# A reordered prologue in a linear-attention plus MLP kernel: tile transposes by DMA, early weight transposes, small loads on ACT's queue

## The chip, the cores and the metric

The kernel runs on one core of one Trainium2 chip. The metric is the device time of one execution in microseconds (us). All matmul inputs are bf16. The engines are PE (TensorE; PEld is its weight load), DVE (VectorE), ACT (ScalarE), POOL (GpSimd) and SP (SyncE), which here only issues DMAs. "SPq" and "ACTq" in the profile are DMA issues in the instruction streams of SP and ACT. Executions of one kernel do not all agree here: the kernel before has runs at about 185.8, 187.5 and 189 us, so runs carry a state (slow when a run is over 1.5% above the fastest of the same kernel, else fast), and comparisons use fast runs.

## The reference, cut to what matters

S = 2048 rows, D = 448 columns, H = 16 heads of 28, F = 1792. Branch A is linear attention with a softmax feature map, branch B a gated mixer and an MLP. Both start from the layer norm of the same x.

```python
xn = _layernorm(x)
# A: q, k, v = xn @ wqkv; per head pq = q @ w_phi, pk = k @ w_phi; phi = [softmax(p), softmax(-p)]
#    kv = phi_k^T v;  o = (phi_q kv) / (phi_q z + 1e-6);  A = o @ wo
# B: h = gelu(layernorm(xn) @ w1); shift four column groups along S; x1 = xn + hs @ w2
#    B = x1 + gelu(layernorm(x1) @ w3) @ w4
return x + A + B
```

The kernel folds w_phi into the q and k parts of wqkv: wpk = wk @ blockdiag(w_phi), and wpq likewise. For that it needs the q and k weights transposed (by DMA transposes from DRAM) and w_phi as a block-diagonal tile `bd` in SBUF.

## The kernel before

Each engine plays its own operations in order.

The prologue before the first exponential works in 16 tiles of 128 rows. It loads, normalizes (statistics on DVE, the power on POOL), transposes each tile into `xnT`, and computes V, the first MLP matmul (w1, gelu) and the folds.

```python
        R.ew(pool, "memset", bd[:, :], 0.0)
        load_x(0, 1)
        load_x(1, 1, "ACT")
        ...
        load_lap(wv, A_wqkv[:, 896:1344], ("ACT", "SP"))
        load_x(4, 2)
        load_x(6, 2)
        load_x(8, 4)
        load_x(12, 4)
        for q in range(4):                       # four loads of 6.1 KB, all on SP
            R.dma(bd[DH * q:DH * q + DH, :].rearrange("e (c f) -> e c f", c=NC)[:, :, DH * q:DH * q + DH],
                  A_w_phi.rearrange("(c q) e f -> q e c f", q=4)[q])
        for t in (1, 0):                         # weight transposes
            for c in range(NC):
                e0 = t * D + CR * c
                R.dma_t(wT[:, t, c, 0:D], A_wqkv[:, e0:e0 + 128])
        ...
        load_lap(w1, B_w1, ("ACT", "ACT"))
        ...
        def xn_T(i, b):                          # PE transpose of a tile, evacuated by ACT
            ...
        def xn_Td(i):                            # DMA transpose of a tile, issued by SP
            R.dma_t(xnT[:, :, 128 * i:128 * i + 128], xn[:, i, :])
```

Tiles 0 to 11 go through `xn_T`, tiles 12 to 15 through `xn_Td`. A list `play([...])` sets the order on PE: `V` are V matmuls, `W` are w1 matmuls, `FO` are folds, `v_out` evacuates V, and `spin` are matmuls that only keep PE busy. Each `W` or `FO` first half fills PSUM banks, and the second half finishes them and is evacuated.

The softmax here doesn't subtract the row's maximum and nothing guards it: scores larger than these inputs give would overflow.

Of the kernel before, what the change touches and what calls it, by code (L numbers as in the profile page):

```python
# [5 lines left out]
ACT = mybir.ActivationFunctionType  # L6
# [217 lines left out]
def bass_parallel_sum__linear_kernel_hedgehog__mixer_s_mlp__prompt_kernel(  # L224
    nc, A_x, A_wqkv, A_w_phi, A_wo, B_x, B_w1, B_w2, B_w3, B_w4, out,
):
    _, S, D = A_x.shape
    H, DH = A_w_phi.shape[0], A_w_phi.shape[1]
    F = B_w3.shape[1]
    assert (S, D, H, DH, F) == (2048, 448, 16, 28, 1792)  # L230
    NT, NG, KC, NC, NM, FC, HP = 16, 4, 4, 4, 4, 14, 32
    CR = 112
# [5 lines left out]
    with es:  # L238
        R = Recorder(nc, es)
# [17 lines left out]
        for b in range(4):  # L257
            t = es.enter_context(nc.psum_tensor("bank%d%d" % (2 * b, 2 * b + 1), [128, 1024], F32))
            R.track(t, 4096, psum=True)
            pairs.append(t)  # L260
        banks = [pairs[b // 2][:, 512 * (b % 2):512 * (b % 2) + 512] for b in range(8)]
# [7 lines left out]
        hT = view(hT_r, NM * HW).rearrange("p (m s) -> p m s", m=NM)  # L269
# [11 lines left out]
        wpk = new("wpk", KC * D).rearrange("p (c d) -> p c d", c=KC)  # L281
# [8 lines left out]
        bd = view(g_r, D)  # L290
# [50 lines left out]
        def load_x(i, n, eng="SP"):  # L341
            R.dma(xtok[:, i:i + n, :], x2d[128 * i:128 * (i + n), :].rearrange("(j p) d -> p j d", p=128), eng)
# [5 lines left out]
        def load_lap(dst, src, engs=("SP", "SP")):  # L348
            for h in range(2):
                R.dma(dst[:, 2 * h:2 * h + 2, :], src[192 * h:192 * h + 256, :].rearrange("(c p) d -> p c d", p=128), engs[h])  # L350
# [6 lines left out]
        load_lap(wv, A_wqkv[:, 896:1344], ("ACT", "SP"))  # L357
        load_x(4, 2)
        load_x(6, 2)
        load_x(8, 4)  # L360
        load_x(12, 4)
        for q in range(4):
            R.dma(bd[DH * q:DH * q + DH, :].rearrange("e (c f) -> e c f", c=NC)[:, :, DH * q:DH * q + DH],
                  A_w_phi.rearrange("(c q) e f -> q e c f", q=4)[q])
        for t in (1, 0):
            for c in range(NC):
                e0 = t * D + CR * c
                R.dma_t(wT[:, t, c, 0:D], A_wqkv[:, e0:e0 + 128])

        def load_rest():  # L370
            R.dma(w2[0:CR, :, :], B_w2.rearrange("(m p) d -> p m d", p=CR))
            load_lap(w3, B_w3)
            load_lap(wo, A_wo)
            R.dma(w4[:, :, :], B_w4.rearrange("(c p) d -> p c d", p=128))
# [2 lines left out]

        R.op("ACT", lambda e: e.preload_act_table_set("gelu_apprx_tanh_and_others"), [], [])
        load_lap(w1, B_w1, ("ACT", "ACT"))
        R.ew(pool, "memset", ident[:, :], 0.0)  # L380
        R.op(pool, lambda e: e.affine_select(ident[:, :], ident[:, :], pattern=[[-1, 128]],
                                             compare_op=ALU.not_equal, fill=1.0, base=0, channel_multiplier=1),
# [8 lines left out]
        def late_3():  # L391
            R.ew(pool, "memset", kvq[:, :, :], 0.0)
            R.ew(pool, "memset", wpq.rearrange("p c (h e) -> p (c h) e", e=HP)[:, :, DH:HP], 0.0)
            R.ew(pool, "memset", phik.rearrange("p t g e -> p (t g) e")[:, :, DH:HP], 0.0)
# [31 lines left out]
        def ln1_stats(a, n, neg):  # L426
            for i in range(a, a + n):
                ln_stats(st, mv, xtok, i)
            ln_scale(mv, rs, a, n, neg)

        def ln1_apply(eng, i):
            ln_apply(eng, halves(xn[:, i, :]), lap(xtok[:, i, :]), mv, rs, i)
# [7 lines left out]
        def fold_pair(t, m, b):  # L440
            def side(k, hi):
                r, c0, c1 = (slice(64, CR), 2 * DH, CR) if hi else (slice(0, 64), 0, 3 * DH)
                return [(banks[2 * b + k][:, CR * c + c0:CR * c + c1],
                         wT[r, t, c, START[m + k]:START[m + k] + 128], bd[r, CR * c + c0:CR * c + c1])
                        for c in range(NC)]

            def late():
                row_pairs(side(1, 0), side(0, 1))
                for k in range(2):
                    a = banks[2 * b + k]  # L450
                    if t:
                        R.ew(dve, "tensor_copy", wpk[:, m + k, :], a[:, 0:D])
                        continue
                    for j in range(2):
                        R.ew(dve, "tensor_copy",
                             wpq[:, m + k, :].rearrange("p (c j h e) -> p c j h e", c=NC, j=2, h=2)[:, :, j, :, 0:DH],
                             a[:, 224 * j:224 * j + 224].rearrange("p (c h e) -> p c h e", c=NC, h=2))
            return lambda: row_pairs(side(0, 0), side(1, 1), True), late
# [9 lines left out]
        def xn_Td(i):  # L468
            R.dma_t(xnT[:, :, 128 * i:128 * i + 128], xn[:, i, :])

        def two(b):
            return pairs[b // 2].rearrange("p (b e) -> p b e", b=2)
# [3 lines left out]
        def row_pairs(first, second, start=False):  # L476
            for s, (p, q) in enumerate(zip(first, second)):
                for out, lhs, rhs in (p, q):
                    R.mm(out, lhs, rhs, start and s == 0, False)

        def lap_pair(outs, lhs, rhs):
            def side(k, rows, kcs):
                return [(outs[k], lhs(k, kc, *rows), rhs(k, kc, *rows)) for kc in kcs]
            return (lambda: row_pairs(side(0, LO, (0, 1, 2, 3)), side(1, HI, (0, 1, 2, 3)), True),
                    lambda: row_pairs(side(1, LO, (0, 1, 3)), side(0, HI, (0, 2, 3))))
# [11 lines left out]
        def v_pair(i, b):  # L497
            return lap_pair([banks[2 * b + k][:, 0:D] for k in range(2)],
                            lambda k, kc, lo, hi: xnT[lo:hi, kc, 128 * (i + k):128 * (i + k) + 128],
                            lambda k, kc, lo, hi: wv[lo:hi, kc, :])  # L500
# [7 lines left out]
                R.ew(dve, "tensor_copy", vd, vs)  # L508

        def w1_pair(g, m, b):  # L510
            p = lap_pair([banks[2 * b + k][0:CR, :] for k in range(2)],
                         lambda k, kc, lo, hi: w1[lo:hi, kc, CR * (m + k):CR * (m + k) + CR],
                         lambda k, kc, lo, hi: xnT[lo:hi, kc, 512 * g:512 * g + 512])

            def late():
                p[1]()
                R.act(hT[0:CR, m:m + 2, 2 + 512 * g:2 + 512 * g + 512], two(2 * b)[0:CR, :, :], ACT.Gelu_apprx_tanh)
            return p[0], late

        def w2_pair(i, b):  # L520
            def side(k, lo, hi):
# [178 lines left out]
        def play(fs):  # L700
            for f in fs:
                f[0](*f[1:])

        for i in range(8):
            ln1_stats(i, 1, 0)
            if i not in (0, 4):
                ln1_apply(dve, i - 1)
            if i == 3:
                ln1_apply(dve, 3)

        def ln1_two(i):
            ln1_stats(i, 2, 1)
            ln1_apply(pool, i)
            ln1_apply(dve, i - 1)

        ln1_two(8)
        ln1_two(10)

        def ln1_rest():
            ln1_two(12)  # L720
            ln1_two(14)
            ln1_apply(dve, NT - 1)
            for i in range(12, 16):
                xn_Td(i)
            load_rest()
            late_3()

        vps = {i: v_pair(i, b) for i, b in ((0, 2), (2, 3), (4, 3), (6, 2), (8, 3), (10, 2))}
        wps = {(g, m): w1_pair(g, m, b) for g, m, b in ((0, 0, 0), (0, 2, 1), (1, 0, 0), (1, 2, 1), (2, 0, 0),
                                                        (2, 2, 1), (3, 0, 0), (3, 2, 3))}  # L730
        fps = {(t, m): fold_pair(t, m, b) for t, m, b in ((1, 0, 2), (1, 2, 3), (0, 0, 2), (0, 2, 1))}

        def V(i, k):
            return (vps[i][k],)

        def W(g, m, k):
            return (wps[g, m][k],)

        def FO(t, m, k):
            return (fps[t, m][k],)  # L740

        spin(19, 256)
        play([(xn_T, 0, 0), (spin, 4, 128), (xn_T, 1, 1), V(0, 0), (xn_T, 2, 0), V(0, 1), (v_out, 0, 2), (xn_T, 3, 1),
              V(2, 0), W(0, 0, 0), V(2, 1), (v_out, 2, 3), (xn_T, 4, 2), W(0, 2, 0), (xn_T, 5, 3), W(0, 0, 1),
              (xn_T, 6, 2), W(0, 2, 1), (xn_T, 7, 3),
              V(4, 0), V(6, 0), V(4, 1), (v_out, 4, 3), V(6, 1), (v_out, 6, 2, "DVE"), (ln1_rest,),
              W(1, 0, 0), (xn_T, 8, 3), W(1, 2, 0), (xn_T, 9, 2), W(1, 0, 1), (xn_T, 10, 3), W(1, 2, 1), (xn_T, 11, 2),
              V(8, 0), V(10, 0), V(8, 1), (v_out, 8, 3), V(10, 1), (v_out, 10, 2, "DVE"),
              W(2, 0, 0), W(2, 2, 0), W(2, 0, 1), FO(1, 0, 0), W(2, 2, 1), FO(1, 2, 0), FO(1, 0, 1), FO(0, 2, 0),
              FO(1, 2, 1), FO(0, 0, 0), FO(0, 2, 1), W(3, 0, 0), FO(0, 0, 1), W(3, 2, 0), W(3, 0, 1), W(3, 2, 1)])  # L750

        def w2_norm(i):
            for j in (i, i + 1):
# [7 lines left out]
        for ps in range(8):  # L761
            k, q = k_pair(2 * ps, 1), q_pair(ps // 2, 2 * (ps % 2), 0)
            kind, i = side[ps]
# [115 lines left out]
```

## Time and profile before

| | kernel before |
|---|---|
| time, median of 3 runs before the prediction | 187.62 us (187.59 to 189.05) |
| span of the profiled run | 184.9 us |
| PE busy | 173.3 us, 94% |
| ACT's first activation (timeline) | 5.84 us |
| first exponential (timeline) | 41.06 us |

These are lines of the profile's page of the kernel before: the span, busy time by engine, and the busy tenths of PE and the granted PE clock in tenths of full speed, in 40 slices of 4.6 us.

```profile
span 184.9 us, 5069 instructions
PE 173.3 (94%) x2193; PEld 101.1 (55%) x2193; DVE 112.6 (61%) x282; ACT 81.7 (44%) x91; POOL 96.5 (52%) x140
PE   7787879899999999999999999999999999999993
PEclk9879999999999999999999999999999999999999
```

Apart from the last slice, every slice in which PE is busy for less than 90% is among the first eight, the prologue. Behind it PE is nearly full, so what the prologue loses or wins moves the end of the kernel.

The windows view of the kernel before gives, for PE in each stretch (us): length, busy time and instructions, granted clock, DMA share and GB/s.

```profile
6.00:9.00 3.00, 2.22 (x25) 0.79 1.07 370
9.00:12.00 3.00, 2.08 (x22) 0.65 0.58 192
```

The clock is halved for one stretch of 3.4 us, from 7.96 to 11.37 us in the trace's clock records.

The timeline of the kernel before shows start, length, engine, line, operation, output <- input; in brackets the idle time before and what ended it.

```profile
2.18 1.00 ACTq L221 DMA_DIRECT2D w<-in_B_w_dram  x2
4.87 10.26 SPq L221 DMA_DIRECT2D g_tok<-in_A_w_phi_dram  x4
5.84 0.60 ACT L211 ACTIVATE xnT<-bank 128x512 bf16<-128x512 bf16 x1 [2.40 <-PE bank L207]
15.17 11.16 SPq L218 DMA_TRANSPOSE hi<-in_A_wqkv_dram  x8
41.06 1.73 ACT L211 ACTIVATE phik<-bank 128x896 bf16<-128x896 f32 x2
```

And this is a line of the waits of SP's DMA queue: who waited for what, us in total, times, longest.

```profile
SPq L221 <- DMA g_tok<-in_A_w_phi_dram: 8.7, 3, 6.3
```

The tile `bd` lives in the buffer `g_tok`. The four small w_phi loads occupy SP's stream for 10.26 us, though one issue takes only about 0.32 us: 8.7 us of it are waits of each load for the one before. The loads write disjoint partitions (0-27, 28-55, 56-83, 84-111), but neighbours share a 32-byte grain and a 64-partition block, so the tracker orders them.

### The profile page before, as it was taken

To read this page: it belongs to the slowest core of one execution; us is meant where nothing else is said; L and a number is where in the kernel's file an instruction comes from. 1 tells how busy PE (TensorE), PEld (TensorE's weight loads), DVE (VectorE), ACT (ScalarE), POOL (GpSimd) and SP (SyncE) were. 2 spreads that over 40 slices of the span, in tenths; PEclk is the share of its full clock that TensorE was granted. 3 is DMA by queue.
4 is the path that set the end of the run, shared out by engine and by line. 5 is a ranking of instruction groups with operands and counts; after the bars stand their busy time and mean duration, and the time that the engine had idled before them with its cause. 6 is when DMAs were issued, how large, how long until landed. Compare 5 with 4: busy or idle time off the path is not lost.

```text
span 184.9 us, 5069 instructions
## 1 busy us (share of the span) xinstructions
PE 173.3 (94%) x2193; PEld 101.1 (55%) x2193; DVE 112.6 (61%) x282; ACT 81.7 (44%) x91; POOL 96.5 (52%) x140
## 2 busy tenths in 40 slices
PE   7787879899999999999999999999999999999993
PEld 5344445695566977666544555455554545545451
DVE  5796183758889969762477695452744527464521
ACT  2248382489976977683524332221322214224000
POOL 3667158002869989993054938762170621722740
PEclk9879999999999999999999999999999999999999
DMA  5931444898000111113001346212622120211321
GB/s 130 362 107 31 96 80 91 270 386 302 8 5 0 32 28 32 28 32 85 0 4 32 59 88 57 78 32 78 88 58 80 30 78 4 82 28 28 82 82 48
DMA packets 33022, 14.88 MB, mean 80 GB/s; under 512 B 24744, under 2 KB 32488, under 8 KB 33000
## 3 DMA queue, kind: packets, MB, share of 16 engines
q1 hardware_dynamic: 31752, 13.58, 29.4%
q10 hardware_dynamic: 1248, 0.98, 1.6%
q8 instruction: 17, 0.28, 0.6%
q14 instruction: 5, 0.04, 0.1%
HBM read 7.08 MB, written 1.84 MB: 48 GB/s over the span
## 4 chain that ended last, share of the span: by engine, by line
PE 75%; DVE 13%; ACT 7%; issue 2%; POOL 1%; DVEq 0%
PE bank L203 75%; ACT hT L211 4%; DVE xn L215 4%; DVE st L215 4%; DVE ksum L215 2%; ACT phik L211 1%; DVE mv L215 1%; ACT xnT L211 1%; POOL rs L215 1%; DVE rks L215 1%; DVE vaug L215 1%; ACT L211 1%; POOL mv L215 0%; PE bank L207 0%; DVEq L176 0%
## 5 line engine op out<-in xcount | busy, mean ns | idle before, releaser
L211 ACT ACTIVATE phik<-bank 128x1024 bf16<-128x1024 f32 (+1 forms) x44 | 42.4, 986 | 61.6 <-PE bank L203 61.6
L203 PE MATMUL bank<-gT,w 64*128 64x512 bf16 x392 | 50.5, 377 | 0.5 <-ACT phik L211 0.2
L215 DVE TENSOR_TENSOR vaug<-bank,vaug 128x464 f32<-128x464 f32 (+3 forms) x65 | 32.6, 512 | 24.0 <-PE bank L203 22.3
L203 PE MATMUL bank<-w,phik 64*128 64x448 bf16 (+1 forms) x420 | 45.0, 349 | 0.1
L215 POOL TENSOR_TENSOR xnT<-vaug 128x196 bf16<-128x196 f32 (+1 forms) x32 | 18.1, 585 | 47.6 <-DVE vaug L215 47.6
L203 PEld LDWEIGHTS bank<-w,phik 64*128 64x128 bf16 (+1 forms) x420 | 21.7, 94 | 21.7 <-PE bank L203 0.5
L215 POOL TENSOR_TENSOR phik<-phik,rks 128x896 bf16<-128x896 bf16 x16 | 26.8, 1699 | 9.9 <-DVE rks L215 9.9
L203 PEld LDWEIGHTS bank<-gT,w 64*128 64x128 bf16 x392 | 18.4, 94 | 18.3 <-ACT phik L211 1.6
L203 PE MATMUL bank<-wv,xnT 64*128 64x448 bf16 x112 | 15.2, 375 | 4.8 <-ACT xnT L211 4.4
L215 DVE TENSOR_REDUCE ksum<-phik 128x32 f32<-128x896 bf16 x16 | 16.8, 1049 | 0.0
L215 POOL TENSOR_TENSOR vaug<-xn,xtok 128x448 f32<-128x448 bf16 x16 | 16.2, 1030 | 1.2 <-DVE vaug L215 1.2
L215 DVE TENSOR_TENSOR xn<-bank,xn 128x256 bf16<-128x256 f32 (+1 forms) x32 | 10.2, 382 | 10.7 <-PE bank L203 10.7
L203 PE MATMUL bank<-w,hT 64*128 64x448 bf16 (+1 forms) x128 | 16.3, 349 | 0.2 <-DVE xn L215 0.2
L203 PE MATMUL bank<-xnT,wpq 64*128 64x512 bf16 x112 | 15.9, 376 | 0.0
L215 DVE RECIPROCAL vaug<-bank 128x16 f32<-128x16 f32 x16 | 4.1, 257 | 17.9 <-PE bank L203 17.9
L203 PE MATMUL bank<-wpk,xnT 64*128 64x448 bf16 x112 | 14.6, 349 | 0.1
L203 PE MATMUL bank<-xnT,w 64*112 64x512 bf16 x112 | 14.4, 380 | 0.0
L203 PE MATMUL bank<-wo,xnT 64*128 64x448 bf16 (+1 forms) x106 | 13.4, 349 | 0.0
L215 POOL TENSOR_SCALAR g_tok<-xn,rs 128x512 bf16<-128x512 bf16 x16 | 12.1, 768 | 0.2
L215 POOL TENSOR_TENSOR rs<-mv,mhalf 128x1 f32<-128x1 f32 (+2 forms) x16 | 11.3, 705 | 1.3
L203 PEld LDWEIGHTS bank<-wv,xnT 64*128 64x128 bf16 x112 | 5.8, 97 | 10.6 <-ACT xnT L211 5.8
L203 PEld LDWEIGHTS bank<-w,hT 64*128 64x128 bf16 (+1 forms) x128 | 9.1, 94 | 4.4 <-DVE xn L215 1.2
(60 smaller groups left out, 181.1 us busy)
## 6 DMA issues: line engine op xcount, KB each, us to landing
w<-in_B_w_dram SPq DMA_DIRECT2D x2, 896.0 KB, 7.3
out_dram<-vaug SPq DMA_DIRECT2D x15, 112.0 KB, 1.9
w<-in_B_w_dram SPq DMA_DIRECT2D x1, 1568.0 KB, 11.2
xtok<-in_A_x_dram SPq DMA_DIRECT2D x2, 448.0 KB, 7.6
xtok<-in_A_x_dram SPq DMA_DIRECT2D x2, 224.0 KB, 6.1
w<-in_B_w_dram ACTq DMA_DIRECT2D x2, 224.0 KB, 6.3
wo<-in_A_wo_dram SPq DMA_DIRECT2D x2, 224.0 KB, 8.4
w<-in_B_w_dram SPq DMA_DIRECT2D x1, 392.0 KB, 3.8
```

Of the source, the lines that this page charges most:

```text
L203: self.op("PE", lambda e: e.matmul(out, lhsT, rhs, start=start, stop=stop, skip_group_check=True), [out], [lhsT, rhs], tile=self._tile(lhsT))
L211: self.op("ACT", lambda e: e.activation(out, in_, func, **kw), [out], [in_] + aps)
L215: self.op(eng, lambda e: getattr(e, name)(out, *args, **kw), [out], aps)
```

## The change

The intent: all of tiles 8 to 15 are transposed by DMA, which takes four transposes and four evacuations from PE and ACT; the weight transposes start early, so the folds can move forward; ACT's evacuations come in the order in which they are needed; and spins fill the first gaps. To free SP for the early transposes, the w_phi loads and x 8-11 move to ACT's queue. This is the core of the diff (bank numbers and the long play list are cut):

```diff
         load_x(6, 2)
-        load_x(8, 4)
-        load_x(12, 4)
-        for q in range(4):
-            R.dma(bd[DH * q:DH * q + DH, :]. ... ,
-                  A_w_phi.rearrange("(c q) e f -> q e c f", q=4)[q])
-        for t in (1, 0):
+        def load_wT(t):
             for c in range(NC):
                 ...
+        load_wT(1)
+        load_x(12, 4)
+        load_wT(0)
 ...
         load_lap(w1, B_w1, ("ACT", "ACT"))
+        for q in range(4):
+            R.dma(bd[DH * q:DH * q + DH, :]. ... ,
+                  A_w_phi.rearrange("(c q) e f -> q e c f", q=4)[q], "ACT")
+        load_x(8, 4, "ACT")
 ...
-                    if t:
-                        R.ew(dve, "tensor_copy", wpk[:, m + k, :], a[:, 0:D])
+                if t:
+                    R.act(wpk[:, m:m + 2, :], two(2 * b)[:, :, 0:D], ACT.Copy)
 ...
-        for i in range(8): ...        # layer norms 8-15 two tiles at a time (ln1_two)
-        def ln1_two(i):
-            ln1_stats(i, 2, 1); ln1_apply(pool, i); ln1_apply(dve, i - 1)
+        for i in range(NT):           # one tile at a time
+            by_pool = i >= 8 and i % 2 == 0
+            ln1_stats(i, 1, int(by_pool))
+            if by_pool:
+                ln1_apply(pool, i)
+            if i and not (i > 8 and i % 2):
+                ln1_apply(dve, i - 1)
+        ln1_apply(dve, NT - 1)
+        for i in range(8, NT):
+            xn_Td(i)
 ...
         spin(19, 256)
-        play([(xn_T, 0, 0), (spin, 4, 128), (xn_T, 1, 1), V(0, 0), ...
+        play([(xn_T, 0, 0), (spin, 3, 256), (xn_T, 1, 1), (spin, 2, 256), V(0, 0), ...
```

The order of ACT's instructions in the changed kernel, as built (not a profile), shows the w_phi loads and their waits ahead of the first evacuation. D19 to D21 are the completions of the first three:

```
5 L221 DMACopy g_tok<-in_A_w_phi_dram 28x4x28 [waits s_POOL]
6 L221 DMACopy g_tok<-in_A_w_phi_dram 28x4x28 [waits s_D19]
7 L221 DMACopy g_tok<-in_A_w_phi_dram 28x4x28 [waits s_D20]
8 L221 DMACopy g_tok<-in_A_w_phi_dram 28x4x28 [waits s_D21]
9 L221 DMACopy xtok<-in_A_x_dram 128x4x448
10 L211 Activation xnT<-bank01 128x4x128 [waits s_PE]
```

More of the change, by code (lines that the diff above doesn't have):

```diff
@@ L359, in bass_parallel_sum__linear_kernel_hedgehog__mixer_s_mlp__prompt_kernel @@
         load_x(6, 2)
-        load_x(8, 4)
-        load_x(12, 4)
-        for q in range(4):
-            R.dma(bd[DH * q:DH * q + DH, :].rearrange("e (c f) -> e c f", c=NC)[:, :, DH * q:DH * q + DH],
-                  A_w_phi.rearrange("(c q) e f -> q e c f", q=4)[q])
-        for t in (1, 0):
+        def load_wT(t):
             for c in range(NC):
@@ L379, in bass_parallel_sum__linear_kernel_hedgehog__mixer_s_mlp__prompt_kernel @@
         load_lap(w1, B_w1, ("ACT", "ACT"))
+        for q in range(4):
+            R.dma(bd[DH * q:DH * q + DH, :].rearrange("e (c f) -> e c f", c=NC)[:, :, DH * q:DH * q + DH],
+                  A_w_phi.rearrange("(c q) e f -> q e c f", q=4)[q], "ACT")
+        load_x(8, 4, "ACT")
         R.ew(pool, "memset", ident[:, :], 0.0)
@@ L448, in late @@
                 row_pairs(side(1, 0), side(0, 1))
+                if t:
+                    R.act(wpk[:, m:m + 2, :], two(2 * b)[:, :, 0:D], ACT.Copy)
+                    return
                 for k in range(2):
                     a = banks[2 * b + k]
-                    if t:
-                        R.ew(dve, "tensor_copy", wpk[:, m + k, :], a[:, 0:D])
-                        continue
                     for j in range(2):
@@ L510, in w1_pair, with w1_out @@
         def w1_pair(g, m, b):
-            p = lap_pair([banks[2 * b + k][0:CR, :] for k in range(2)],
+            return lap_pair([banks[2 * b + k][0:CR, :] for k in range(2)],
                          lambda k, kc, lo, hi: w1[lo:hi, kc, CR * (m + k):CR * (m + k) + CR],
                          lambda k, kc, lo, hi: xnT[lo:hi, kc, 512 * g:512 * g + 512])
-            def late():
-                p[1]()
-                R.act(hT[0:CR, m:m + 2, 2 + 512 * g:2 + 512 * g + 512], two(2 * b)[0:CR, :, :], ACT.Gelu_apprx_tanh)
-            return p[0], late
+        def w1_out(g, m, b):
+            R.act(hT[0:CR, m:m + 2, 2 + 512 * g:2 + 512 * g + 512], two(2 * b)[0:CR, :, :], ACT.Gelu_apprx_tanh)
         def w2_pair(i, b):
@@ L702, in play @@
                 f[0](*f[1:])
-        for i in range(8):
-            ln1_stats(i, 1, 0)
-            if i not in (0, 4):
-                ln1_apply(dve, i - 1)
-            if i == 3:
-                ln1_apply(dve, 3)
-        def ln1_two(i):
-            ln1_stats(i, 2, 1)
-            ln1_apply(pool, i)
-            ln1_apply(dve, i - 1)
-        ln1_two(8)
-        ln1_two(10)
-        def ln1_rest():
-            ln1_two(12)
-            ln1_two(14)
-            ln1_apply(dve, NT - 1)
-            for i in range(12, 16):
-                xn_Td(i)
-            load_rest()
-            late_3()
-        vps = {i: v_pair(i, b) for i, b in ((0, 2), (2, 3), (4, 3), (6, 2), (8, 3), (10, 2))}
-        wps = {(g, m): w1_pair(g, m, b) for g, m, b in ((0, 0, 0), (0, 2, 1), (1, 0, 0), (1, 2, 1), (2, 0, 0),
-                                                        (2, 2, 1), (3, 0, 0), (3, 2, 3))}
-        fps = {(t, m): fold_pair(t, m, b) for t, m, b in ((1, 0, 2), (1, 2, 3), (0, 0, 2), (0, 2, 1))}
+        for i in range(NT):
[4 more added lines that the diff above has]
+            if i and not (i > 8 and i % 2):
+                ln1_apply(dve, i - 1)
+        ln1_apply(dve, NT - 1)
+        for i in range(8, NT):
+            xn_Td(i)
+        load_rest()
+        late_3()
+        vps = {i: v_pair(i, b) for i, b in ((0, 2), (2, 3), (4, 3), (6, 2), (8, 2), (10, 3))}
+        wps = {(g, m): w1_pair(g, m, b) for g, m, b in ((0, 0, 0), (0, 2, 1), (1, 0, 0), (1, 2, 1), (2, 0, 2),
+                                                        (2, 2, 0), (3, 0, 2), (3, 2, 3))}
+        fps = {(t, m): fold_pair(t, m, b) for t, m, b in ((1, 0, 0), (1, 2, 1), (0, 0, 3), (0, 2, 1))}
         def V(i, k):
@@ L742, in bass_parallel_sum__linear_kernel_hedgehog__mixer_s_mlp__prompt_kernel @@
         spin(19, 256)
-        play([(xn_T, 0, 0), (spin, 4, 128), (xn_T, 1, 1), V(0, 0), (xn_T, 2, 0), V(0, 1), (v_out, 0, 2), (xn_T, 3, 1),
-              V(2, 0), W(0, 0, 0), V(2, 1), (v_out, 2, 3), (xn_T, 4, 2), W(0, 2, 0), (xn_T, 5, 3), W(0, 0, 1),
-              (xn_T, 6, 2), W(0, 2, 1), (xn_T, 7, 3),
-              V(4, 0), V(6, 0), V(4, 1), (v_out, 4, 3), V(6, 1), (v_out, 6, 2, "DVE"), (ln1_rest,),
-              W(1, 0, 0), (xn_T, 8, 3), W(1, 2, 0), (xn_T, 9, 2), W(1, 0, 1), (xn_T, 10, 3), W(1, 2, 1), (xn_T, 11, 2),
-              V(8, 0), V(10, 0), V(8, 1), (v_out, 8, 3), V(10, 1), (v_out, 10, 2, "DVE"),
-              W(2, 0, 0), W(2, 2, 0), W(2, 0, 1), FO(1, 0, 0), W(2, 2, 1), FO(1, 2, 0), FO(1, 0, 1), FO(0, 2, 0),
-              FO(1, 2, 1), FO(0, 0, 0), FO(0, 2, 1), W(3, 0, 0), FO(0, 0, 1), W(3, 2, 0), W(3, 0, 1), W(3, 2, 1)])
+        play([(xn_T, 0, 0), (spin, 3, 256), (xn_T, 1, 1), (spin, 2, 256), V(0, 0), (xn_T, 2, 0), V(0, 1), (xn_T, 3, 1),
+              (spin, 2, 256), V(2, 0), (v_out, 0, 2), W(0, 0, 0), V(2, 1), (v_out, 2, 3), W(0, 2, 0), (xn_T, 4, 2), W(0, 0, 1),
+              (xn_T, 5, 2), W(0, 2, 1), (xn_T, 6, 2), V(4, 0), (xn_T, 7, 2), V(4, 1), (w1_out, 0, 0, 0), V(6, 0), (w1_out, 0, 2, 1),
+              (v_out, 4, 3), W(1, 0, 0), V(6, 1), (v_out, 6, 2), W(1, 2, 0), W(1, 0, 1), (w1_out, 1, 0, 0), W(1, 2, 1),
+              (w1_out, 1, 2, 1), V(8, 0), FO(1, 0, 0), V(8, 1), (v_out, 8, 2), FO(1, 2, 0), FO(1, 0, 1), FO(1, 2, 1),
+              V(10, 0), W(2, 0, 0), V(10, 1), (v_out, 10, 3), W(2, 2, 0), FO(0, 2, 0), W(2, 0, 1), (w1_out, 2, 0, 2),
+              FO(0, 0, 0), W(2, 2, 1), (w1_out, 2, 2, 0), FO(0, 2, 1), W(3, 0, 0), FO(0, 0, 1), W(3, 2, 0),
+              W(3, 0, 1), (w1_out, 3, 0, 2), W(3, 2, 1), (w1_out, 3, 2, 3)])
         def w2_norm(i):
```

## The prediction

> **What bounds the kernel.** PE is busy 173.3 of 184.9 us (page, busy table). From 42.8 us on it has almost no gaps: 138.2 us busy of 142.2 (windows view). The change touches only the prologue up to the first exponentials at 41.06 us (timeline). From 5 to 42.8 us PE is busy 31.3 of 37.8 us, so at most 6.5 us of idling, plus about 1.7 us lost to the half clock (granted clock 0.79 and 0.65 between 6 and 12 us), can be won. The chain of waits runs over layer norms until 15.4 us, then over alternating ACT evacuations (0.60 us transposes, 1.02 us gelus) and PE.
>
> **What the change removes.** Four PE transposes of tiles (8 matmuls, 0.29 us each, 1.2 us of PE) with four ACT evacuations (0.60 us each, 2.4 us); two DVE casts of V (1.09 us) and four of wpk (0.58 us) move to ACT, as 2 x 0.92 us and about 2 x 0.95 us. Evacuations of tiles 4-7 no longer stand behind gelus, layer norms 12-15 no longer behind V casts; the SP queue issues the weight transposes (1.2-1.3 us each) from about 3.5 instead of 15.2 us. Alone this might win 3 us.
>
> **What it adds.** The four small w_phi loads move from the SP queue to ACT, ahead of ACT's first evacuation. Each waits for the landing of the one before: the instruction order shows the waits in ACT's stream. Before, these waits held SP 8.7 us (6.3 + 1.2 + 1.2; waits view of the DMA queue). The Trainium skill, "DMA: Bandwidth & Descriptors", Anatomy of one DMA, says that not DMA engines but the issuing sequencer waits on semaphores; the trace agrees, SP issued nothing meanwhile. Now ACT stands still. The first load lies behind w1 on ACT's queue, whose data end at 9.1 us (DMA records); the dependent loads then take about 1.5 us each. ACT issues the fourth near 12.3, then x 8-11, and makes its first evacuation near 13 us instead of 5.84. PE needs two evacuations for its first V matmul: about 14.3 instead of 7.0 us. After that idling the clock should be halved for 3 to 6 us (Trainium skill, "TensorE: Matmul & The Clock Gate", Part 1: an idle window of about 3.4 us throttles; this trace shows one).
>
> **Sum (estimates from trace durations).** PE work left at 14.3 us: 6 transposes 1.8, V 6 x 1.41, w1 8 x 1.63, folds 4 x 0.8 = 26.5 us; plus 2 us half clock, plus 1 us waits on ACT/DVE (wpq copies 0.31 us each before the last w1 pair): the last w1 matmul ends at 43.8 instead of 38.4 us. Behind it PE is the bound and the delay is kept. Predicted +5.3 us: 193 us, range 189.5 to 196. Chances: faster by over 2% 0.08, within 2% 0.20, slower by over 2% 0.72.
>
> **What would show it.** Right: ACT's first activation at 12-14.5 us, waits of ACT's queue on w_phi landings of 8-9 us, a PE gap of 5 us or more from about 7 us, clock 0.5 somewhere in 10-20 us, first exponential at 45-47.5 us, a rigid shift after. Transposes of tiles 8-15 land in time. Wrong: first activation before 8 us, PE dense from 7 us, first exponential before 39 us.
>
> **What would make it wrong.** Landings of w_phi faster than on SP; gaps in the new order smaller than I count; or tile transposes landing late, which would make it worse.

## More of the kernel before

A `Recorder` collects every operation in program order, with the bytes it reads and writes, and works out the semaphore waits.

The part that matters here is how the bytes are named: 32-byte grains in a row, but only two blocks of 64 partitions.

```python
GRAIN = 32
...
        p0 = (ap.offset * esz) // row_bytes
        p1 = p0 + dims[0][1]
        halves = [h for h in (0, 1) if p0 < 64 * h + 64 and p1 > 64 * h]
        keys = set()
        for s in starts:
            for b in range(s // GRAIN, (s + run - 1) // GRAIN + 1):
                for h in halves:
                    keys.add((name, b, h))
...
            for fn, todo, src, dma in self.stream[eng]:
                for f, i in todo:
                    e.wait_ge(get(f), 16 if f[0] == "D" and f[1:].isdigit() else self.marked[f][i])
                ins = fn(e)
```

## The result, and the profile after

The changed kernel takes 194.22 us (median of 4 runs, 194.14 to 195.13); the kernel before took 187.61 us in the same rounds (186.14 to 189.05). The ratio is 1.0391, 95% interval 1.0321 to 1.046. Here and below a ratio is the mean time of one kernel's fast runs over that of the other's fast runs of the same rounds, so not quite the ratio of the medians.

The page of the changed kernel, the same lines as before (slices are 4.8 us):

```profile
span 192.3 us, 5016 instructions
PE 175.4 (91%) x2164; PEld 101.4 (53%) x2164; DVE 110.1 (57%) x276; ACT 83.0 (43%) x91; POOL 99.1 (52%) x148
PE   7304999989999999999999999999999999999994
PEclk9855699999999999999999999999999999999999
```

PE is busy for 0.3, 0.0 and 0.4 of slices 2 to 4, and the clock is low from the third slice to the fifth. From there on the two kernels look alike. The windows of the changed kernel say the same in us:

```profile
6.00:9.00 3.00, 0.83 (x13) 0.94 1.45 260
9.00:12.00 3.00, 0.00 (x0) 0.50 1.06 201
12.00:15.00 3.00, 0.00 (x0) 0.50 0.82 198
15.00:19.00 4.00, 1.87 (x12) 0.50 0.58 142
19.00:23.00 4.00, 4.00 (x37) 0.59 0.03 8
```

The timeline of the changed kernel, with the lines that answer to those shown of before:

```profile
3.16 6.13 SPq L218 DMA_TRANSPOSE hi<-in_A_wqkv_dram  x4
3.24 12.76 ACTq L221 DMA_DIRECT2D g_tok<-in_A_w_phi_dram  x4
16.48 1.08 ACT L211 ACTIVATE xnT<-bank 128x512 bf16<-128x512 bf16 x2 [13.04 <-DMA g_tok<-in_A_w_phi_dram]
17.13 2.16 PE L203 MATMUL bank<-wv,xnT 64*128 64x448 bf16 x8 [9.97 <-ACT xnT L211]
48.53 1.73 ACT L211 ACTIVATE phik<-bank 128x896 bf16<-128x896 f32 x2
```

The four loads hold ACT from 3.24 to 16.0 us. ACT's first evacuation comes at 16.48 instead of 5.84 us, and PE, which has nothing to multiply before two tiles are evacuated, stands for 9.97 us. The first exponential is 7.47 us later than before (48.53 against 41.06), and so is the end: the spans differ by 7.4 us. (The medians differ by 6.6 us; the profiled run of the kernel before took 187.03 us, a little less than its median.)

The chain that ended last, in the changed kernel (start, length, what), follows exactly these landings:

```profile
3.24 7.43 DMA g_tok<-in_A_w_phi_dram
10.69 3.16 DMA g_tok<-in_A_w_phi_dram
13.87 1.78 DMA g_tok<-in_A_w_phi_dram
16.48 0.60 ACT xnT L211
```

### The profile page after: what moved, and what is told of

It is laid out like the page before. It is cut to its first block, busy times and chain, and to the rows that moved or that the text cites. A ratio compares the mean times of both kernels' runs of the same rounds, so it can differ in the third digit from the quotient of the medians.

```text
span 192.3 us, 5016 instructions
## 1 busy us (share of the span) xinstructions
PE 175.4 (91%) x2164; PEld 101.4 (53%) x2164; DVE 110.1 (57%) x276; ACT 83.0 (43%) x91; POOL 99.1 (52%) x148
## 3 DMA queue, kind: packets, MB, share of 16 engines
q1 hardware_dynamic: 32896, 13.62, 29.5%
## 4 chain that ended last, share of the span: by engine, by line
PE 78%; DVE 8%; DMA 6%; ACT 4%; ACTq 1%; issue 1%; DVEq 0%
PE bank L203 77%; DMA g_tok<-in_A_w_phi_dram 6%; DVE xn L215 3%; DVE ksum L215 2%; ACT phik L211 1%; ACT hT L211 1%; ACTq L221 1%; DVE st L215 1%; PE bank L207 1%; DVE rks L215 1%; DVE wpq L215 1%; ACT L211 1%; ACT xnT L211 1%; DVE mv L215 0%; ACT L378 0%
## 5 line engine op out<-in xcount | busy, mean ns | idle before, releaser
L203 PE MATMUL bank<-wv,xnT 64*128 64x448 bf16 x112 | 16.3, 385 | 10.3 <-ACT xnT L211 10.0
L203 PE MATMUL bank<-xnT,w 64*112 64x512 bf16 x112 | 14.9, 381 | 1.1 <-DVE wpq L215 1.0
L203 PEld LDWEIGHTS bank<-wv,xnT 64*128 64x128 bf16 x112 | 6.5, 99 | 15.7 <-ACT xnT L211 11.2
L215 DVE BATCH_NORM_STATS2 st<-xtok 128x6 f32<-128x448 bf16 x16 | 9.8, 615 | 7.5 <-DMA xtok<-in_A_x_dram 7.5
L215 POOL TENSOR_TENSOR rs<-mv,mhalf 128x1 f32<-128x1 f32 (+1 forms) x20 | 12.9, 644 | 1.7
```

What stands on the lines that cost most here:

```text
L203: self.op("PE", lambda e: e.matmul(out, lhsT, rhs, start=start, stop=stop, skip_group_check=True), [out], [lhsT, rhs], tile=self._tile(lhsT))
L215: self.op(eng, lambda e: getattr(e, name)(out, *args, **kw), [out], aps)
```

## The experiments

Theory A: the chained loads in ACT's instruction stream are the loss. Rival B: the new order itself (banks, evacuations moved to ACT, tile transposes by DMA) costs the time. Theory C came up on the way: a short PE wait costs more than its length, because the half clock follows it. Every run was numerically correct. Each kernel that was timed in rounds was compared with runs of the kernel before on the same chip; medians of those runs were 187.18, 187.55 and 187.52 us in the three sets.

### 1. The changed kernel without the chain (a_nochain)

The loads write disjoint partitions, so the tracker only has to see that. This takes no true dependence away; every other wait of the changed kernel stays, except that the folds now wait on all four loads.

```diff
-GRAIN = 32
+GRAIN = 32; CUTS = ((0, 28), (28, 56), (56, 64), (64, 84), (84, 128))
-        halves = [h for h in (0, 1) if p0 < 64 * h + 64 and p1 > 64 * h]
+        halves = [h for h, (a, b) in enumerate(CUTS) if p0 < b and p1 > a]
```

> The changed kernel, with the four w_phi loads on ACT's queue made independent of one another (they write disjoint partitions; only the dependence tracker's 64-row blocks chained them). Theory A (the chained loads hold ACT's instruction stream): ACT's first activation at 5.5 to 6.5 us instead of 16.5, first V matmul near 7 us, first exponential at 38 to 39.5 us instead of 48.5, time 184 to 186.5 us, so below the kernel before. Rival B (the new order itself, with its bank turns, its evacuations on ACT or its late tile transposes, costs the time and the stall is recovered): ACT starts early, but the time stays above 189 us, with the PE gaps moved to later waits.

Measured: 188.07 us (187.06 to 189.42), ratio to the kernel before 1.0075 (1.0004 to 1.0146). This is some 6 us below the changed kernel (two sets of rounds), but no win over the kernel before. Both theories were half right. The stall is gone, but the timeline shows a new wait later, and the windows show what follows it:

```profile
6.65 1.09 ACT L211 ACTIVATE xnT<-bank 128x512 bf16<-128x512 bf16 x2 [3.21 <-POOL mv L215]
17.26 13.20 SPq L218 DMA_TRANSPOSE xnT<-xn  x8
31.93 1.19 PE L203 MATMUL bank<-xnT,w 64*112 64x512 bf16 x8 [2.55 <-DMA xnT<-xn]
41.60 0.92 ACT L211 ACTIVATE phik<-bank 128x896 bf16<-128x896 f32 x1
```

```profile
28.00:32.00 4.00, 1.45 (x28) 1.00 0.23 42
32.00:36.00 4.00, 3.21 (x23) 0.59 0.99 354
36.00:40.00 4.00, 4.00 (x24) 0.55 1.05 390
```

PE runs out of work near 29.4 us and waits 2.55 us for the last tile transpose. Layer norm 15 ended only at 29.2 us. Two things make it late. With one tile at a time DVE waits for POOL's power and POOL for DVE's statistics (3.0 us for two tiles). And the last step, DVE's write of xn for tile 15, took 2.57 us, where the same instruction takes 0.41 us for tiles 9, 11 and 13; it ran beside three POOL memsets (26.58 to 29.10 us), which follow POOL's last power in program order, and ended 0.14 us after them:

```profile
26.67 2.57 DVE L215 TENSOR_SCALAR xn<-xtok,mv,rs 128x512 bf16<-128x512 bf16 x1 [1.79 <-POOL rs L215]
27.30 1.80 POOL L215 MEMSET phik<- 128x2048 bf16 x1
```

SP had issued the seventh tile transpose by 27.25 us and could issue the last only at 29.27 us. With a write of 0.41 us it could have issued it at 27.3 us. So by estimate about 2.0 of the 2.55 us are due to that one slow write, and only the rest to the chain of layer norms. The changed kernel shows the same (2.57 us from 32.46 us), but there PE came later and did not have to wait. Then the clock is at one half from 33.0 to 39.8 us, with PE busy for all but 0.8 us of it.

### 2. The kernel before without the chain (b_nochain)

The same two lines changed in the kernel before.

> The kernel before, with the same four loads made independent on the SP queue. Theory A: in the kernel before the chain held SP only, and nothing on the chain of waits came from SP's weight transposes, so the time stays within 1 us of the kernel before (186.5 to 188.5), while the weight transposes are issued near 6.5 us instead of 15.2. If instead it falls by 2 us or more, the gain of the independent loads in the changed kernel would not be the rest of the change but the early weight transposes.

Measured: 187.13 us (185.81 to 188.99), ratio 0.9996 (0.9929 to 1.0064), with the weight transposes issued from 6.84 instead of 15.17 us. As expected: on SP the chain was harmless, and early weight transposes alone win nothing.

### 3. The kernel before with only the chained loads on ACT (b_phi_act)

```diff
-        for q in range(4):
-            R.dma(bd[...], A_w_phi...[q])
 ...
         load_lap(w1, B_w1, ("ACT", "ACT"))
+        for q in range(4):
+            R.dma(bd[...], A_w_phi...[q], "ACT")
```

> The kernel before, with only the four chained w_phi loads moved to ACT's queue behind w1, as the change does. Theory A: this alone is the loss: ACT's first activation near 14 to 16 us, first exponential near 49 to 52 us, time 195 to 198 us, slower than the changed kernel by about 2 to 3 us (what the rest of the change gains). Rival B: time within 2 us of the kernel before, since its order would recover the stall.

Measured: 198.59 us (198.32 to 200.22), ratio 1.0652 (1.0585 to 1.0719). ACT's first activation is at 16.00 us. The time is above the 195 to 198 us expected, and the profiled run is the slowest of the four. This one part of the change costs more than the whole change, so the rest of it wins back about 2.5% while the stall is there (1.0652 over 1.0391, two different sets of rounds). The waits view of this run shows for PE why the old order recovers less: it alternates with ACT, five waits on tile evacuations, where the changed kernel has only the one of 9.97 us.

```profile
PE bank L203 <- ACT xnT L211: 14.0, 5, 9.8
```

### 4. Control: the same loads on ACT, but independent (b_act_ind)

Run 3 with the finer blocks of run 1.

> Control: the kernel before, with the w_phi loads on ACT's queue as in the run that took 198.6 us, but independent of one another. If the chain of waits is the whole loss and not the queue or the issue work on ACT: ACT's first activation between 5.8 and 6.6 us and 186.5 to 188.5 us, as the kernel before. If issuing on ACT costs by itself, above 190 us.

Measured: 188.83 us (187.31 to 189.41), ratio 1.0046 (0.9979 to 1.0112); the median is a little above the expected band. The timeline:

```profile
3.23 3.06 ACTq L221 DMA_DIRECT2D g_tok<-in_A_w_phi_dram  x4
6.34 1.19 ACT L211 ACTIVATE xnT<-bank 128x512 bf16<-128x512 bf16 x2 [2.90 <-POOL rs L215]
```

Issuing the loads costs ACT 3.06 us, in which it had little else to do. Runs 2, 3 and 4 together pin it: the chain on SP is free, the loads on ACT are nearly free, and only the chain on ACT costs some 11 us (6%, 1.0652 over 1.0046, two sets of rounds).

### 5 and 6. Keeping PE busy through the stall (a_spin, a_spin2)

```diff
-(spin, 2, 256), V(0, 0), (xn_T, 2, 0)
+(spin, 88, 256), V(0, 0), (xn_T, 2, 0)      # a_spin;  104 in a_spin2
```

> The changed kernel with 88 instead of 2 spin matmuls of 256 columns before the first V pair, so that PE is busy through ACT's stall and the clock stays full. Theory A with my estimate for the clock (2 us lost to the half clock): granted clock 1.0 from 12 to 22 us, ACT's first activation unchanged at 16.5 us, first exponential 1.5 to 2.5 us earlier than in the changed kernel (46 to 47 us), time 192 to 193 us. If the half clock costs nothing because PE waits for ACT there anyway, the time stays within 0.5 us of the changed kernel.

Measured with 88 spins: 195.37 us (195.15 to 196.17), ratio to the kernel before 1.0469 (1.0417 to 1.0521): no gain, about 1 us more than the changed kernel, and a badly sized experiment. The chain of loads took 14.29 us in this run instead of 12.76, so ACT came at 18.01 us; the spins had ended 1.9 us before PE could go on, and the clock was halved from 20.6 to 24.0 us all the same. So a longer one was run.

> The changed kernel with 104 spin matmuls before the first V pair instead of 2 (88 ended before ACT was released, and the clock was halved from 20.6 to 24.0 us all the same). If the clock stays full throughout, the stretch from ACT's first activation to the first exponential, 32.05 us in the changed kernel and 31.56 us with 88 spins, shows what the half clock cost: 30 us if my 2 us were right, 31.5 us or more if PE waited for ACT there anyway. Time 194 to 196 us, as the chain's length varies.

Measured with 104 spins (one run, state unknown): 194.05 us, clock full from 6.3 us on. The timeline:

```profile
18.13 1.09 ACT L211 ACTIVATE xnT<-bank 128x512 bf16<-128x512 bf16 x2 [14.69 <-DMA g_tok<-in_A_w_phi_dram]
48.44 1.73 ACT L211 ACTIVATE phik<-bank 128x896 bf16<-128x896 f32 x2
```

From ACT's first activation to the first exponential it takes 30.31 us, against 32.05 us in the changed kernel (48.53 less 16.48). The half clock cost about 1.7 us there, by one profiled run of each. The total time does not show it, because in this run ACT was released 1.65 us later (18.13 against 16.48). Why the chain is longer in both spin kernels stays open.

### 7. Spins in the later gap (a_gap_spin)

Run 1 plus 22 pairs of 64-row spins in front of the w1 pair that waits for the last tile.

```diff
+        def spin_rows(n, b):
+            for _ in range(n):
+                for k, (lo, hi) in enumerate((LO, HI)):
+                    R.mm(banks[2 * b + k][:, 0:256], busy[lo:hi, 0:128], busy[lo:hi, 0:256], True, True)
-FO(0, 2, 1), W(3, 0, 0),
+FO(0, 2, 1), (spin_rows, 22, 2), W(3, 0, 0),
```

> The kernel with independent w_phi loads (188.1 us), plus 22 pairs of 64-row spin matmuls between the last early fold and the w1 pair of tiles 12-15, where PE stood 2.5 us on the last tile transposes; after that wait the clock was halved from 33.0 to 39.8 us. If the half clock is what eats the gain (theory C), the clock stays at 1.0 after 30 us, the w1 and k matmuls behind the gap run at full speed and the time falls by 2.5 to 3.5 us to 184.5 to 185.7 us, although PE does not get its data any earlier. If the late data alone matter (rival), the time stays at 187.5 to 188.5 us.

Measured: 186.38 us (186.11 to 187.17), ratio 0.9972 (0.9909 to 1.0034); 1.7 us below run 1 by medians of two sets of rounds, less than expected, and the two intervals overlap; the profiles say more. The clock was full, and the timeline says why the gain is smaller: PE could start on the last tiles 1.2 us later than in run 1 (33.13 against 31.93; the last transpose was issued at nearly the same time, but took 1.3 us longer to land), and still the first exponential came earlier, at 40.70 instead of 41.60 us.

```profile
29.20 2.58 PE L203 MATMUL bank<-gT 64*128 64x256 bf16 x44 [0.16 <-ACT hT L211]
33.13 1.07 PE L203 MATMUL bank<-xnT,w 64*112 64x512 bf16 x8 [1.35 <-issue]
```

From there to the first exponential it took 7.57 us with the full clock (40.70 less 33.13) and 9.67 us with the half clock (41.60 less 31.93). So in the profiled runs the half clock behind the gap cost 2.1 us. Theory C holds, with a smaller number than I gave.

### 8. Layer norms in pairs (a_ln)

Run 1 plus the old way to do layer norms 8 to 15:

```diff
-        for i in range(NT):
-            by_pool = i >= 8 and i % 2 == 0
-            ...
+        for i in range(8):
+            ln1_stats(i, 1, 0)
+            if i:
+                ln1_apply(dve, i - 1)
+        for i in range(8, NT, 2):
+            ln1_stats(i, 2, 1)
+            ln1_apply(pool, i)
+            ln1_apply(dve, i - 1)
         ln1_apply(dve, NT - 1)
```

> The kernel with independent w_phi loads, with layer norms 8-15 done two tiles at a time as in the kernel before (one power for two tiles, the DVE's apply one pair later), all eight tiles still transposed by DMA. I expect the last layer norm near 23.5 instead of 29.2 us; then the SP queue's own 1.26 us per transpose is the limit: last landing near 29.7 to 30.2 instead of 31.7 us, PE's wait 0.5 to 1.2 us instead of 2.5, no half clock, time 183.5 to 185.5 us. If the clock is halved still, about 186.5 us.

Measured: 184.45 us (182.87 to 185.98), ratio 0.9834 (0.9743 to 0.9925). In the profiled run (182.87 us) PE waits for no tile transpose and the clock stays full; the first exponential is at 36.90 us. So what kept run 1 from winning was the lateness of layer norm 15 behind the DMA transposes. Which of its causes matters more is not tested: this run takes away both that run 1 shows. Layer norm 15 ends at 22.17 instead of 29.24 us; its DVE write takes 0.41 instead of 2.57 us, as POOL's memsets now start after it. The eight tile transposes then follow one another on SP without a wait, and the last is issued at 26.06 us. That is 3.2 us earlier than in run 1, of which 2.0 us, by the estimate given there, are the slow write. Another 1.0 us is that the first transpose was issued earlier (16.29 against 17.26 us), which differs from run to run. So little is left for the saved hand-overs between DVE and POOL. A run with one tile at a time and the memsets moved would test this; there is none.

```profile
21.76 0.41 DVE L215 TENSOR_SCALAR xn<-xtok,mv,rs 128x512 bf16<-128x512 bf16 x1 [0.94 <-POOL rs L215]
```

The profiled run is also the fastest of the four. The other three (one of them slow) have a mean clock of 0.98 to 0.99, so a stretch at half clock came back in them. What is left of PE's waits there is DVE's copying of wpq (timeline of the profiled run):

```profile
31.31 0.42 PE L203 MATMUL bank<-xnT,w 64*112 64x512 bf16 x1 [0.79 <-DVE wpq L215]
```

### 9. As 8, with tiles 14 and 15 transposed by PE (a_fix)

`xn_Td` for tiles 8 to 13 only; `(xn_T, 14, 3)` and `(xn_T, 15, 3)` in the play list, evacuated by DVE; `W(2, 0, 0)` ahead of `V(10, 0)`.

> As the run before in this list (independent w_phi loads, layer norms in pairs), and tiles 14 and 15 transposed by PE with their evacuation on DVE, so that six transposes are left on the SP queue. I expect no wait of PE for a tile transpose, no half clock after 12 us, first exponential near 35.5 us instead of 41.6, and 181.5 to 183.5 us, faster than the kernel before by 2 to 3%.

Measured: 184.36 us (183.2 to 184.58), ratio 0.9837 (0.9755 to 0.9918). There is no wait for DMA transposes and no half clock in any of its four runs, but no gain over run 8 by the median either: the profiled run has the first exponential at 38.57 us, 1.67 us later than in run 8. That fits x 8-11, which reached DVE 1.68 us later (14.08 us against 12.40 us in the profiled run 8); a PE transpose also waited 0.5 us on its layer norm. My 35.5 us was wrong, and so were the 181.5 to 183.5 us.

### 10. Weight transposes out of the way (a_wT_late)

The changed kernel, chain kept, but on SP all x loads come first and the weight transposes only behind the first tile transpose:

```diff
-        load_wT(1)
+        load_x(8, 4)
         load_x(12, 4)
-        load_wT(0)
 ...
+        xn_Td(8)
+        load_wT(1)
+        load_wT(0)
-        for i in range(8, NT):
+        for i in range(9, NT):
             xn_Td(i)
```

> The changed kernel with its chained w_phi loads on ACT, but with the weight transposes on the SP queue put behind the first tile transpose (near 18 us), so that none runs beside the chain, and all x loads on SP ahead of them. If the weight transposes slowed the chain (it took 12.8 us; I had predicted about 9.5), ACT's first activation comes at 12.5 to 13.5 us instead of 16.5, with waits of about 6, 1.5 and 1.5 us. If it is x 12-15 or the queue itself, it stays near 16. The total time is not the point; late weight transposes delay the folds, so 190 to 197 us.

Measured (one run, state unknown): 195.08 us. The timeline:

```profile
3.24 10.77 ACTq L221 DMA_DIRECT2D g_tok<-in_A_w_phi_dram  x4
14.05 1.08 ACT L211 ACTIVATE xnT<-bank 128x512 bf16<-128x512 bf16 x2 [10.62 <-POOL mv L215]
```

Here the bracket names POOL, which had long been done; the wait was for the loads. The chain took 10.77 us, 2.0 us less than in the changed kernel; ACT's 14.05 us is still later than the 12.5 to 13.5 us expected. This run also moved x 8-11 to SP, but run 3 tells the two moves apart: its x loads are on SP at the same times (3.16 and 3.67 us), its weight transposes start at 4.46 us beside the chain, and its chain took 12.73 us. So the change's own early transposes lengthened the chain that it had put on ACT; that explains about 2.0 us of the 3.5 us by which I had mis-sized it, by one profile of each (the chain took 12.73 to 14.42 us in the four profiles that have transposes beside it).

### 11 and 12. The best version (a_best), and it without one move (a_ln2)

Run 8 plus query folds placed earlier (both kernels), and x 8-11 loaded on SP ahead of the weight transposes (a_best only):

```diff
+        load_x(8, 4)                      # a_best only
         load_wT(1)
 ...
-        load_x(8, 4, "ACT")               # a_best only
 ...
-              V(10, 0), W(2, 0, 0), V(10, 1), (v_out, 10, 3), W(2, 2, 0), FO(0, 2, 0), W(2, 0, 1), (w1_out, 2, 0, 2),
-              FO(0, 0, 0), W(2, 2, 1), (w1_out, 2, 2, 0), FO(0, 2, 1), W(3, 0, 0), FO(0, 0, 1), W(3, 2, 0),
+              V(10, 0), W(2, 0, 0), V(10, 1), (v_out, 10, 3), FO(0, 2, 0), W(2, 0, 1), (w1_out, 2, 0, 2), FO(0, 2, 1),
+              W(2, 2, 0), FO(0, 0, 0), W(2, 2, 1), (w1_out, 2, 2, 0), FO(0, 0, 1), W(3, 0, 0), W(3, 2, 0),
```

> Independent w_phi loads, layer norms 8-15 in pairs, and two more moves: x 8-11 loaded on the SP queue ahead of the weight transposes, and the query folds put earlier, so that the DVE's wpq copies (2.66 us, PE waited 0.8 + 0.2 us on them) are done before the last w1 pairs. I expect x 8-11 landed by 11 us, no PE wait on wpq, first exponential near 36 us, 182 to 184 us in most runs, and less spread than the 182.9 to 186.0 us of the kernel with layer norms in pairs alone.

> As the run before in this list but with x 8-11 still on ACT's queue behind w_phi. If only the fold order matters: about 1 us below the kernel with layer norms in pairs alone (184.5 us), so 183 to 184 us. If the landing of x 8-11 (12.4 to 14.1 us in the two profiles so far) is what spreads the times, this one still spreads by 2 us or more and the run before does not.

Measured: a_best takes 181.79 us (181.61 to 182.8, six runs), ratio 0.9695 (0.9644 to 0.9746). It is faster than both kernels, by 3% than the one before. a_ln2 takes 183.69 us (182.52 to 185.94), ratio 0.9753 (0.9693 to 0.9814), with two of its six runs slow; its profile fell into a slow run and is not read here. The waits of PE in a_best up to 90 us, all that the view lists:

```profile
PE bank L203 <- DVE gT L215: 1.2, 1, 1.2
PE bank L203 <- DVE xn L215: 0.5, 2, 0.2
PE bank L203 <- ACT phik L211: 0.2, 1, 0.2
PE bank L207 <- DVE xn L215: 0.2, 1, 0.2
```

Only the start-up (1.2 us until DVE has set the spin operand) is longer than 0.2 us. The first exponential comes at 36.01 us, 5.05 us before that of the kernel before. That only the early x 8-11 removes the spread agrees with the theory that their landing spread the times, but one pair of kernels is thin evidence.

## Why the prediction was right or wrong

The time, 194.22 us, lies in the range of 189.5 to 196 us, near the 193 us given, and the direction is right. The number is nearer than its terms: the first exponential moved by 7.47 instead of 5.3 us, as the stall ended 2.8 us later for PE than predicted and the work behind it took 0.7 us less. Of the signs that the prediction named, the PE gap (9.97 us), the half clock and the rigid shift came; ACT's first activation, the first exponential and the waits of ACT's queue (11.0 us instead of 8 to 9) lie outside their ranges. The steps:

- **"Now ACT stands still."** Right, and shown twice: taking the chain away removes some 6 us from the changed kernel (run 1), and adding only it to the kernel before costs some 11 us (runs 3 and 4). The Trainium skill, "DMA: Bandwidth & Descriptors", Anatomy of one DMA, says that the issuing sequencer waits, not the DMA engine (in a section on DMAs issued by GpSimd); the trace agrees for ACT, with 13.04 us of idle ACT.
- **The length of the stall.** Mis-sized. "First evacuation near 13 us": it came at 16.48 us. I had let the first load land soon after 9.1 us, where w1's data ended in the kernel before, and had taken 1.5 us per dependent load from an undisturbed SP queue. The chain measured 7.43, 3.16 and 1.78 us, start to landing, so the first landed at 10.69 us, and it and the second load make up nearly all of the error. Run 10 puts about 2.0 us on the weight transposes beside the chain; the rest is not settled.
- **PE's first V matmul "about 14.3"**: 17.13 us, 2.8 us late by the same error. The first exponential, predicted at 45 to 47.5 us, came at 48.53 us for the same reason.
- **The sum behind it.** Right: 29.5 us predicted from there to the end of the last w1 matmul (14.3 to 43.8), 28.8 us measured (17.13 to 45.90). In it, the 2 us for the half clock: 1.7 us by runs 5 and 6. ("Halved for 3 to 6 us": the clock records have it at half from 8.87 to 22.52 us, but PE worked only in the last 5.4 us of that.) The 1 us for waits on wpq: 1.0 us in PE's waits.
- **"Behind it PE is the bound and the delay is kept."** Right: 7.47 us at the first exponential, 7.4 us at the end of the span.
- **"Alone this might win 3 us."** Wrong as the change was written: without the stall it was not faster than the kernel before (1.0075). The failed step is **"Transposes of tiles 8-15 land in time"**. They did in the changed kernel, but only because the stall had made PE late. Once PE ran early it waited 2.55 us for the last of them and then 6.8 us at half clock. I had left out that layer norms done one tile at a time pass between DVE and POOL twice as often, and that the last of them then runs on DVE beside POOL's memsets (2.57 instead of 0.41 us); that the second costs more (about 2.0 of the 2.55 us) is an estimate from run 1, not a test. With pairs restored, the loads independent and the loads and folds reordered, the change is worth 5.7 us (a_best, ratio 0.9695).

## What to carry to other kernels

Before a DMA is moved to a compute engine's queue, look at what that DMA waits for: an engine plays its stream in order, and a wait that is free on an idle queue becomes a stall on a busy one. Dependence trackers that round to blocks create such waits between loads that never touch the same bytes. When a large stall is removed, look for the next thing that was hidden behind it, and count a PE wait of 2 to 3 us as more than its length, since the clock may be halved afterwards. Compare how long one and the same instruction takes in the two kernels, too: the slow DVE write showed only that way.

## What the Trainium skill lacked or had wrong

- "TensorE: Matmul & The Clock Gate", the closing table, advises no PE-idle gaps over about 3 us between matmul bursts. In run 1 a wait of 2.55 us was enough: the clock was halved for 6.83 us, from 33.0 to 39.8 us, twice the 3.41 us of the shortest stretch seen; in run 5 one of 1.9 us was (3.41 us at half). Of short idling the page says that it can do the same, but gives no figure: in the kernel before, PE was busy for 2.06 us of the 3.41 us from 4.55 to 7.96 us, with no gap above 0.6 us, and 3.41 us at half clock followed.
- "DMA: Bandwidth & Descriptors", Issuing engines are not separate DMA queues, says that issuing from several engines only saves the sequencer's time. Run 4 agrees where there is no wait (ratio 1.0046). The same page does say, under Anatomy of one DMA, that the issuing sequencer waits on semaphores; what no page adds is what such a wait costs when the issuing engine also computes: 8.7 us on SP cost nothing, some 11 us on ACT cost PE 9.97 us.
- No page gives a figure for what DMA transposes and ordinary loads cost one another from two queues (that DMAs of several engines interleave is stated). Four 6.1 KB loads in a chain took 10.77 us without (run 10; 10.26 us on SP in the kernel before) and 12.73 to 14.42 us beside weight transposes (the changed kernel, runs 3, 5 and 6). Four weight transposes took 6.13 and then 5.08 us to issue beside the loads, against 10.78 us for eight later on (run 10), so they lost little.
